# Attention and two MLPs on one core: more working rooms, folded key chunks in turns with the others, and 30 instead of 40 steps of the first MLP beside attention

## The chip, the core and the metric

One core of a Trainium2 chip runs the whole program. The metric is device microseconds of one launch (us). TensorE (PE) multiplies matrices, VectorE (DVE) and ScalarE (ACT) work element by element, GpSimd (POOL) and SyncE (SP) mostly issue DMAs here. Each engine takes its instructions in a fixed order that is set when the program is built.

## What is computed

```python
scores = scale * np.matmul(z, z.transpose(0, 2, 1))     # scale = 1 / S
attn = np.maximum(scores, 0.0) ** 2
x = u * np.matmul(attn, v)                              # (2, 3008, 256) -> (6016, 256)

h = x @ w_in                                            # first MLP, 256 -> 2048 -> 256
P = a[0] + a[1] * h + a[2] * h**2 + a[3] * h**3
Q = 1.0 + np.abs(b[0]) * np.abs(h) + np.abs(b[1]) * h**2
x = (P / (Q + 1e-06)) @ w_out

h = x @ w_in2                                           # second MLP, 256 -> 2048 -> 256
out = (np.maximum(h, 0.0) + alpha * np.minimum(h, 0.0)) @ w_out2
```

The MLPs' weights come in 64-bit type and are converted to 32 bits on the core. Every 32-bit operand is split into a high and a low part, and a product is up to three matmuls (high by high, high by low, low by high).

## The kernel before

**Attention.** There are two batches of 3008 rows. The queries of a batch are taken in six blocks j of 512 (the last has 448), the keys in twelve chunks kp of 256 (the last has 192). One attention step is one chunk of one block: 4 matmuls for the scores (L393, L394), relu and square on ACT into a tile r (L397, L400), a split into high and low part (ACT L118, DVE L121), and 12 matmuls with the values (L437, L446), which follow three steps later. There are 2 x 6 x 12 = 144 steps, counted by st. At a block's end DVE multiplies by u (L482) and the product goes to memory.

**Folding.** The scores are symmetric. In the second batch (`FOLD`) a chunk that lies in an earlier block than its queries is not computed anew: its r was computed when the roles were the other way round. `turn_block` turns such an r with two DMA transposes into a tile xt (L333), `save_turned` writes xt to memory (L341), and `load_turned` fetches it for the later block into a tile xd (L351); ACT and DVE put its two 16-bit halves together (L362, L363). Block j of the second batch has 2j folded chunks, which come first, and turns 10 - 2j others. xt and xd have two buffers each (`XT`, `XD`); tiles r, and the scratch tiles sq, ab and t of the first MLP, share the six buffers of tag "t" (`TT`). A folded chunk has no score matmuls.

**MLPs.** The 6016 rows are taken in 12 groups of 512 (the last has 384), the 2048 hidden columns in 8 parts. One step is one group and one part: 12 matmuls into the hidden tile (L417 to L419) and 12 back (L437, L446), 24 in all, for either MLP. In between, the first MLP has five ACT instructions (L561 to L563, L570, L571) and seven DVE instructions (L565 to L578); the second has two ACT instructions (L621) and two DVE instructions (L622) of half the size, and a split (L118, L121). There are 96 steps of each.

**Weights.** They arrive as 64-bit words, are converted on DVE and ACT (`decode`), and all but 8 tiles of the first MLP's are stored again (wd, L217). Beside attention, a first-MLP step with part 4 to 7 needs two fills of 512 KB from there (L774), which POOL issues. When attention ends, 24 tiles are filled, 16 of them into buffers that the values leave.

**Order.** The main loop takes the attention steps one by one and adds a first-MLP step where `n1_due` says so:

```python
def n1_due(st):
    return max(st + 1 - HEAD, 0) * X1 // (na - HEAD)
```

With HEAD = 36, X1 = 40 and na = 145, 13 steps come in the first batch and 27 in the second. After attention, the other 56 first-MLP steps and 86 second-MLP steps go in turn, spread evenly; 10 second-MLP steps are left for the end. A scheduler then fixes each engine's order, and waits are set where a buffer or a value is needed. All transposes, saves and loads of turned chunks, as well as v, z, u and x, go through the one queue of SP.

Of the kernel before, what the change touches and what calls it, by code (L numbers as in the profile page):

```python
# [11 lines left out]
U16 = mybir.dt.uint16  # L12
# [3 lines left out]
DRAM = bass.MemoryType.DRAM  # L16


BIG, HL, TT, RAW, ZP, XP = 24, 7, 6, 2, 8, 4

XT, XD, AHEAD = 2, 2, 1

FOLD = ((1, 0),)

# [3 lines left out]

LAG_A, LAG_M = 3, 2

HEAD, X1 = 36, 40

RD0, RD = 0.4, 0.55

# [18 lines left out]
def relu2_attention_rational_mlp_prelu_mlp(  # L53
# [15 lines left out]
    nc = tc.nc  # L69
    P = 128  # L70
# [6 lines left out]
    QB = 512  # L77
    NQ = -(-S // QB)
    NK = -(-S // P)
    NKP = NK // 2  # L80
# [15 lines left out]
    zctx = ExitStack()  # L96
    zp = zctx.enter_context(tc.tile_pool(name="zp", bufs=ZP))
    wr = zctx.enter_context(tc.tile_pool(name="wr", bufs=WR))
    xdp = zctx.enter_context(tc.tile_pool(name="xdp", bufs=XD))
    late = {}  # L100

    def raw_tile(nm, early=False):

        if early:
            return big.tile([P, 1024], F32, tag="big", name=nm)
        return tmp.tile([P, 1024], F32, tag="raw", name=nm, bufs=RAW)
# [34 lines left out]
    def load_v(b, kp):  # L141

        if b == 0:
            raw = raw_tile("vraw", True)
        else:
            raw = wr.tile([P, 1024], F32, tag="wr", name="vraw")
        r3 = raw.rearrange("p (c d) -> p c d", c=4)
        r0 = kp * 2 * P
        load_rows(r3, v[b], r0, min(S - r0, 4 * P))
        vraw[b, kp] = r3  # L150
# [97 lines left out]
    def load_z(b, g):  # L248

        raw = raw_tile("zraw", b == 0)  # L250
        n = qn[g]
        nc.sync.dma_start(out=raw[:, 0:n], in_=zt[b, :, g * QB : g * QB + n])
        if n % P:
            nc.sync.dma_start(out=raw[:, n : n + HALF], in_=zt[b, :, S - HALF : S])
            n += HALF
        t = zp.tile([P, QB], F32R, tag="z", name="zA")
        with tc.high_priority(EARLY):
            nc.vector.tensor_copy(t[:, 0:n], raw[:, 0:n])
            nc.vector.tensor_tensor(
                t[HALF:P, 0:n], raw[HALF:P, 0:n], t[HALF:P, 0:n].bitcast(F32), ALU.subtract  # L260
            )
        if (b, g) == (0, 0):
            zB[b, g] = zp.tile([P, QB], F32R, tag="z", name="zB")
            nc.scalar.copy(zB[b, g][HALF:P, 0:n], raw[HALF:P, 0:n])
            nc.vector.tensor_tensor(
                zB[b, g][0:HALF, 0:n], raw[0:HALF, 0:n], t[0:HALF, 0:n].bitcast(F32), ALU.subtract
            )
        zA[b, g] = t


    blocks = [(b, j) for b in range(B) for j in range(NQ)]
# [4 lines left out]
    xd = {}  # L276
# [39 lines left out]
    def folded(b, i, j):  # L316
        return i < j and any(b == fb and i >= f0 for fb, f0 in FOLD)

    turned = {}
    halves = {}  # L320
    unsaved = []

    def turn_block(b, j, kp, r):

        kb, k0 = kp // 2, kp % 2 * 2 * P
        if (b, j, kb) not in turned:
            turned[b, j, kb] = dr.tile([2, QB, QB], U16, name=f"rt{b}_{j}_{kb}")
        x = xdp.tile([P, 8, 2 * P], U16, tag="xt", name="xt", bufs=XT)
        ru = r.bitcast(U16)
        w = 0  # L330
        for i in range(2):
            rows = min(P, S - (2 * kp + i) * P)
            nc.sync.dma_start_transpose(out=x[:, :, w : w + rows], in_=ru[0:rows, i, :])  # L333
            w += rows
        unsaved.append((turned[b, j, kb], k0, w, x))
# [10 lines left out]
    def load_turned(b, j, kp):  # L346
        n = qn[j]
        q0 = kp % 2 * 2 * P
        d = xdp.tile([P, 2, 2, QB], U16, tag="xd", name="xd", bufs=XD)
        for h in range(2):  # L350
            nc.sync.dma_start(  # L351
                out=d[:, h, :, :n],
                in_=turned[b, kp // 2, j][h, q0 : q0 + 2 * P, :n].rearrange("(c p) k -> p c k", p=P),
            )
        halves[b, j, kp] = d
# [13 lines left out]
    def a_scores(b, j, kp):  # L369
# [43 lines left out]
        if folded(b, j, kp // 2):  # L413
            turn_block(b, j, kp, r)
# [16 lines left out]
    def pairs(acc, w, hi, lo, n, first, last, both=2):  # L431

        hi, lo = ([x[i] if type(x) is list else x[:, i, :n] for i in range(2)] for x in (hi, lo))
        for i in range(2):
            for e in range(2):
                for k in range(2):
                    nc.tensor.matmul(  # L437
                        acc[:, e, :n],
                        w[:, k, i, e * P : (e + 1) * P],
                        hi[i],  # L440
                        start=first and i == 0 and k == 0,
                        stop=False,
                    )
        for i in range(both):
            for e in range(2):
                nc.tensor.matmul(  # L446
                    acc[:, e, :n],
                    w[:, 0, i, e * P : (e + 1) * P],
                    lo[i],
                    start=False,  # L450
                    stop=last and i == both - 1,
                )

    def a_values(b, j, kp):
        n = qn[j]
        if kp == 0:

            two = j == 1 and not opened
            acc_a[b, j] = psa.tile([P, ND, QB], F32, tag=f"acc{two:d}", name="acca")
        acc = acc_a[b, j]  # L460
        hi, lo = ahl.pop((b, j, kp))
        vk = vt[b, kp]
        last = kp == NKP - 1
        pairs(acc, vk, hi, lo, n, kp == 0, last, 1 if last else 2)

    def a_u(b, j):
        n = qn[j]
        t = tmp.tile([P, ND, QB], F32, tag="raw", name="ut", bufs=RAW)
        if b == 0 and j < RAW:

            nc.gpsimd.tensor_copy(t[:, 0, 0:1], zA[0, NQ - 1][:, 0:1].bitcast(F32))
        nc.sync.dma_start(
            out=t[:, :, :n],
            in_=ut_in[b, :, j * QB : j * QB + n].rearrange("(e p) s -> p e s", p=P),
        )
        uts[b, j] = t

    def a_end(b, j):
        n = qn[j]
        t = uts.pop((b, j))  # L480
        with tc.high_priority(EARLY):
            nc.vector.tensor_tensor(t[:, :, :n], acc_a[b, j][:, :, :n], t[:, :, :n], ALU.mult)  # L482
        xd[b, j] = dr.tile([P, ND, QB], F32, name=f"xd{b}_{j}")
        nc.sync.dma_start(out=xd[b, j][:, :, :n], in_=t[:, :, :n])
# [185 lines left out]
    def a_stream():  # L670

        pend = []
        coming = [(b, j, kp) for b, j in blocks for kp in range(2 * j) if folded(b, kp // 2, j)]

        def fetch(b, j, kp):
            while coming and len(halves) < AHEAD + folded(b, kp // 2, j) and (
                coming[0][:2] == (b, j) or coming[0][:2] == (b, j + 1) and kp >= NKP - 2
            ):
                load_turned(*coming.pop(0))

        def drain(upto):
            while len(pend) > upto:
                q, kp = pend.pop(0)
                a_values(*q, kp)
                if kp == NKP - 2:
                    a_u(*q)
                if kp == NKP - 1:
                    a_end(*q)

        for q in blocks:  # L690
            b, j = q
            if q == (0, 0):
                load_z(0, 0)
                load_z(0, 1)
                load_v(0, 0)
                split_v(0, 0)
            a_begin(b, j)
            for kp in range(NKP):
                if q == (0, 0) and kp % 2 == 0:
                    for g in {0: (2,), 2: (3, 4), 4: (5,)}.get(kp, ()):  # L700
                        load_z(0, g)
                    if kp + 2 < NKP:
                        load_v(0, kp + 2)
                        split_v(0, kp + 2)
                fetch(b, j, kp)
                a_scores(b, j, kp)
                save_turned(int(folded(b, j, kp // 2)))
                pend.append((q, kp))
                drain(LAG_A)
                if j == NQ - 1 and b + 1 < B:  # L710
                    if kp % 2 == 1:
                        load_z(b + 1, kp // 2)

                k0 = kp - LAG_A - 1 if j == NQ - 1 else kp + NKP - LAG_A - 1
                b1 = b + (j == NQ - 1)
                if (j == NQ - 1 or j == 0) and 0 < b1 < B and k0 % 2 == 0:
                    if 0 <= k0 < NKP:
                        split_v(b1, k0)
                    if 0 <= k0 + 2 < NKP:
                        load_v(b1, k0 + 2)  # L720
                yield
        drain(0)
        yield

# [29 lines left out]
    na = NB * NKP + 1  # L754
# [29 lines left out]
            fill_w(store, jp, big)  # L784

    def n1_due(st):
        return max(st + 1 - HEAD, 0) * X1 // (na - HEAD)

    n1 = nx = 0
    for st in range(na):  # L790
# [79 lines left out]
```

## Time and profile before

| | |
|---|---|
| three runs | 1598.0, 1600.2, 1601.96 us |
| median | 1600.2 us |
| profiled execution | 1600.62 us |
| its span, first to last instruction | 1598.7 us |
| PE busy | 1539.4 us, 96% |
| DVE busy | 1413.9 us, 88% |
| ACT busy | 1172.8 us, 73% |
| DMA: from SP's queue | 93.67 MB, 21.8% of 16 engines |
| DMA: from POOL's queue | 62.94 MB, 13.4% of 16 engines |

The span is the time from the first to the last instruction; the execution has 1.9 us around it. Busy time is a share of the span; matmuls overlap, so a busy PE need not be at its peak. In the windows below, the number in parentheses is that of instructions, and the granted clock is a share of 2.4 GHz.

### The profile page before, as it was taken

What the parts mean: (1) busy time and instruction counts of PE and PEld (TensorE: products, weight loads), DVE (VectorE), ACT (ScalarE), POOL (GpSimd) and SP (SyncE); (2) the same over time, 40 slices, a digit from 0 to 9 for tenths busy, and PEclk for the clock granted to TensorE, in tenths of its full rate; (3) what the DMA queues carried; (4) which work ended last, traced back from release to release, by engine and by line L of the source; (5) the groups of instructions that cost most, each with busy time, mean ns of one, the idle gap of its engine ahead of it and who ended that gap; (6) DMA issues with size and microseconds to landing.
All of it is one profiled execution on the core that took longest, in us unless ns stands there. A gap on an engine that the chain in (4) does not pass through costs nothing.

```text
span 1598.7 us, 18271 instructions
## 1 busy us (share of the span) xinstructions
PE 1539.4 (96%) x6776; PEld 1271.4 (80%) x6776; DVE 1413.9 (88%) x1524; ACT 1172.8 (73%) x1405; POOL 90.5 (6%) x159
## 2 busy tenths in 40 slices
PE   9999999998989889888999999999999999999999
PEld 7887888786768667667788888888888888888888
DVE  8989989896979788999999998999989899998864
ACT  8989988897877878777676676667667676666644
POOL 1021000000001001101200000000000000000000
PEclk9999999998999899999999999999999999999999
DMA  6364132569897878676700010100001000001000
GB/s 203 101 208 148 59 106 73 163 148 228 235 210 209 175 221 157 192 197 214 259 2 27 27 40 1 40 12 28 27 27 40 1 27 28 35 1 40 14 1 23
DMA packets 155784, 157.76 MB, mean 99 GB/s; under 512 B 74016, under 2 KB 124720, under 8 KB 155696
## 3 DMA queue, kind: packets, MB, share of 16 engines
q1 hardware_dynamic: 134928, 93.67, 21.8%
q0 software_dynamic: 20768, 62.94, 13.4%
q8 instruction: 53, 0.87, 0.2%
q14 instruction: 35, 0.29, 0.1%
HBM read 92.94 MB, written 45.74 MB: 87 GB/s over the span
## 4 chain that ended last, share of the span: by engine, by line
PE 67%; DVE 11%; issue 9%; DMA 5%; ACT 5%; POOL 1%; SPq 0%; POOLq 0%; DVEq 0%; ACTq 0%
PE acc L437 18%; PE h L417 9%; PE h L419 9%; PE h L418 9%; PE acc L446 9%; PE acca L437 6%; PE acca L446 3%; DVE alo L121 2%; DMA wd<-dec 1%; PE s L393 1%; PE s L394 1%; DMA xt<-r 1%; PE acce L427 1%; DVE t L577 1%; ACT ahi L118 1%
## 5 line engine op out<-in xcount | busy, mean ns | idle before, releaser
L437 PE MATMUL acc<-ghi,w 128*128 128x512 f32 (+1 forms) x1472 | 365.9, 387 | 1.7 <-DVE ghi L575 1.7
L437 PEld LDWEIGHTS acc<-ghi,w 128*128 128x128 f32 x1472 | 275.3, 188 | 57.3 <-DVE ghi L575 1.6
L437 PE MATMUL acca<-ahi,vt 128*128 128x512 f32 (+1 forms) x1152 | 294.8, 394 | 10.5 <-ACT ahi L118 6.9
L417 PE MATMUL h<-xhi,w 128*128 128x512 f32 (+1 forms) x768 | 295.8, 386 | 4.1 <-DVE t L568 2.1
L418 PE MATMUL h<-xlo,w 128*128 128x512 f32 (+1 forms) x768 | 295.7, 385 | 1.1 <-DVE xlo L121 1.1
L419 PE MATMUL h<-xhi,w 128*128 128x512 f32 (+1 forms) x768 | 295.7, 385 | 0.0
L437 PEld LDWEIGHTS acca<-ahi,vt 128*128 128x128 f32 x1152 | 220.2, 192 | 58.4 <-ACT ahi L118 10.5
L446 PE MATMUL acc<-glo,w 128*128 128x512 f32 (+1 forms) x736 | 199.9, 390 | 10.5 <-DVE glo L578 10.3
L621 ACT ACTIVATE m<-h,sal 128x512 f32<-128x512 f32 (+1 forms) x192 | 127.4, 681 | 111.3 <-PE h L419 109.9
L561 ACT ACTIVATE sq<-h 128x1024 f32<-128x1024 f32 (+1 forms) x96 | 97.1, 1011 | 149.7 <-PE h L419 141.0
L417 PEld LDWEIGHTS h<-xhi,w 128*128 128x128 f32 x768 | 144.1, 188 | 35.4 <-issue 4.1
L446 PEld LDWEIGHTS acc<-glo,w 128*128 128x128 f32 x736 | 137.5, 188 | 41.9 <-DVE glo L578 14.9
L418 PEld LDWEIGHTS h<-xlo,w 128*128 128x128 f32 x768 | 144.1, 188 | 29.4 <-DVE xlo L121 1.9
L419 PEld LDWEIGHTS h<-xhi,w 128*128 128x128 f32 x768 | 144.1, 188 | 27.6
L121 DVE TENSOR_TENSOR glo<-m,ghi 128x1024 fp32r<-128x1024 f32 (+1 forms) x96 | 115.2, 1200 | 55.2 <-PE acc L437 42.0
L622 DVE SCALAR_TENSOR_TENSOR m<-h,sg,m 128x512 f32<-128x512 f32 (+1 forms) x192 | 138.1, 735 | 16.8 <-ACT m L621 15.3
L446 PE MATMUL acca<-alo,vt 128*128 128x512 f32 (+1 forms) x552 | 149.9, 389 | 0.0
L121 DVE TENSOR_TENSOR alo<-r,ahi 128x1024 fp32r<-128x1024 f32 (+2 forms) x103 | 122.9, 1195 | 17.9 <-PE acc L437 8.0
L397 ACT ACTIVATE r<-s 128x512 f32<-128x512 f32 (+1 forms) x184 | 104.2, 595 | 42.5 <-DMA xt<-r 24.3
L575 DVE SCALAR_TENSOR_TENSOR ghi<-t,sc,sq 128x1024 fp32r<-128x1024 f32 (+1 forms) x96 | 120.8, 1258 | 13.1 <-ACT sq L571 7.1
L565 DVE SCALAR_TENSOR_TENSOR ab<-sq,cb,ab 128x1024 f32<-128x1024 f32 (+1 forms) x96 | 120.8, 1258 | 9.9 <-ACT ab L562 9.7
L577 DVE SCALAR_TENSOR_TENSOR t<-t,sc,ab 128x1024 f32<-128x1024 f32 (+1 forms) x96 | 120.9, 1260 | 1.8
(96 smaller groups left out, 2222.8 us busy)
## 6 DMA issues: line engine op xcount, KB each, us to landing
w<-wd POOLq DMA_DIRECT2D x64, 512.0 KB, 4.9
rt<-xt SPq DMA_DIRECT2D x50, 256.0 KB, 3.1
wd<-dec POOLq DMA_DIRECT2D x48, 256.0 KB, 4.2
xd<-rt SPq DMA_DIRECT2D x40, 256.0 KB, 3.6
wraw<-in_moe_w_in_dram POOLq DMA_DIRECT2D x16, 512.0 KB, 4.3
wraw<-in_moe_w_out_dram POOLq DMA_DIRECT2D x16, 512.0 KB, 4.5
x2d<-x SPq DMA_DIRECT2D x11, 512.0 KB, 2.9
xr<-x2d SPq DMA_DIRECT2D x11, 512.0 KB, 3.3
```

What stands on the lines that cost most here:

```text
L121: nc.vector.tensor_tensor(dst_lo, src, dst_hi.bitcast(F32), ALU.subtract)
L397: nc.scalar.activation(r[:, i, :n], s, AF.Relu, scale=1.0 / S)
L417: nc.tensor.matmul(acc, w_hi, hi, start=first, stop=False)
L418: nc.tensor.matmul(acc, w_hi, lo, start=False, stop=False)
L419: nc.tensor.matmul(acc, w_lo, hi, start=False, stop=last)
L437: nc.tensor.matmul(acc[:, e, :n], w[:, k, i, e * P : (e + 1) * P], hi[i], start=first and i == 0 and k == 0, stop=False,)
L446: nc.tensor.matmul(acc[:, e, :n], w[:, 0, i, e * P : (e + 1) * P], lo[i], start=False, stop=last and i == both - 1,)
L565: nc.vector.scalar_tensor_tensor(ab, sq, b1, ab, ALU.mult, ALU.add)
L575: nc.vector.scalar_tensor_tensor(hi, t, a0, sq, ALU.add, ALU.mult)
L577: nc.vector.scalar_tensor_tensor(t, t, a0, ab, ALU.add, ALU.subtract)
L621: nc.scalar.activation(t[:, i], h, AF.Copy, scale=sal[:, f : f + 1])
L622: nc.vector.scalar_tensor_tensor(t[:, i], h, sg[:, f : f + 1], t[:, i], ALU.mult, ALU.max)
```

## The change

The tag "t" gets seven buffers instead of six. Tiles xt and xd share one tag "xx" with six buffers, where each had two. The room for this comes from the memory set apart for POOL's DMA descriptors, which is set to 4096 bytes. In a block of the second batch, folded chunks and others come in turns: block 4, for instance, takes 8, 0, 1, 9, 2, 3, 10, 4, 5, 11, 6, 7 where it took 0 to 11. The first MLP gets 16 steps in the first batch and 14 in the second.

```diff
-BIG, HL, TT, RAW, ZP, XP = 24, 7, 6, 2, 8, 4
-XT, XD, AHEAD = 2, 2, 1
+BIG, HL, TT, RAW, ZP, XP = 24, 7, 7, 2, 8, 4
+XX, AHEAD = 6, 1
+RING = 4096
...
-HEAD, X1 = 36, 40
+HEAD, X0, X1 = 36, 16, 30
...
-    xdp = zctx.enter_context(tc.tile_pool(name="xdp", bufs=XD))
+    xdp = zctx.enter_context(tc.tile_pool(name="xdp", bufs=XX))
...
+    def in_turns(b, j):
+        first = [kp for kp in range(NKP) if folded(b, kp // 2, j)]
+        rest = [kp for kp in range(NKP) if kp not in first]
+        order, nf = [], len(first)
+        while first or rest:
+            ahead = len(first) * (NKP - nf) > len(rest) * nf
+            order.append((first if ahead else rest).pop(0))
+        return order
...
-        x = xdp.tile([P, 8, 2 * P], U16, tag="xt", name="xt", bufs=XT)
+        x = xdp.tile([P, 8, 2 * P], U16, tag="xx", name="xt")
...
-        d = xdp.tile([P, 2, 2, QB], U16, tag="xd", name="xd", bufs=XD)
+        d = xdp.tile([P, 2, 2, QB], U16, tag="xx", name="xd")
...
-            for kp in range(NKP):
+            for pos, kp in enumerate(order[q]):
...
     def n1_due(st):
-        return max(st + 1 - HEAD, 0) * X1 // (na - HEAD)
+        mid = NQ * NKP
+        if st < mid:
+            return max(st + 1 - HEAD, 0) * X0 // (mid - HEAD)
+        return X0 + (st + 1 - mid) * (X1 - X0) // (na - mid)
...
-    nc = _bacc.Bacc("TRN2", target_bir_lowering=False, num_devices=1)
+    nc = _bacc.Bacc("TRN2", target_bir_lowering=False, num_devices=1, dynamic_dma_scratch_size=RING)
```

Where the code asked for the first, last or last but one chunk of a block it now asks for the place in that order, and the fetch of folded chunks follows it too. In the changed kernel the transposes are L346, the saves L354, the loads L364; L565, L567, L568, L575 to L578 are L578, L580, L581, L588 to L591, and L622 is L635.

The SP queue in the second batch's first block, where chunks are only turned, stood so before (xt is the turned chunk, r the scores, rt the memory it is saved to, xd a loaded chunk):

```order
L333 DMA_TRANSPOSE xt_3259<-r_3245 128x8x128 x2
L333 DMA_TRANSPOSE xt_3291<-r_3276 128x8x128 x2
L341 DMA rt1_0_2_3185<-xt_3259 64x8x256 x2
L341 DMA rt1_0_3_3290<-xt_3291 64x8x256 x2
L333 DMA_TRANSPOSE xt_3322<-r_3308 128x8x128 x2
L351 DMA xd_3583<-rt1_0_1_3069 128x2x512
L341 DMA rt1_0_3_3290<-xt_3322 64x8x256
L333 DMA_TRANSPOSE xt_3396<-r_3381 128x8x128 x2
L341 DMA rt1_0_3_3290<-xt_3322 64x8x256
L341 DMA rt1_0_4_3395<-xt_3396 64x8x256 x2
```

and stands so now:

```order
L346 DMA_TRANSPOSE xt_3385<-r_3370 128x8x128 x2
L346 DMA_TRANSPOSE xt_3416<-r_3402 128x8x128 x2
L354 DMA rt1_0_3_3384<-xt_3385 64x8x256 x2
L346 DMA_TRANSPOSE xt_3448<-r_3433 128x8x128 x2
L354 DMA rt1_0_3_3384<-xt_3416 64x8x256 x2
L346 DMA_TRANSPOSE xt_3496<-r_3482 128x8x128 x2
L354 DMA rt1_0_4_3447<-xt_3448 64x8x256 x2
L364 DMA xd_3513<-rt1_0_1_3199 128x2x512 x2
L346 DMA_TRANSPOSE xt_3531<-r_3516 128x8x128 x2
L354 DMA rt1_0_4_3447<-xt_3496 64x8x256 x2
```

Before, two chunks are transposed, then both are saved, or a transpose stands behind the save of the chunk before it. Now the transposes of a further chunk stand between a chunk's transposes and its saves.

DVE in the middle of the MLPs, a piece of some twelve instructions before (L567 to L578 are of one first-MLP step; each pair of L622, with a glo<-m, is a second-MLP step):

```order
L567 TENSOR_TENSOR t<-t,h_8251 128x1024
L622 SCALAR_TENSOR_TENSOR m<-h_8295,sg,m 128x512
L622 SCALAR_TENSOR_TENSOR m<-h_8304,sg,m 128x512
L568 SCALAR_TENSOR_TENSOR t<-t,sc,h_8251 128x1024
L575 SCALAR_TENSOR_TENSOR ghi<-t,sc,sq 128x1024
L576 SCALAR_TENSOR_TENSOR ab<-ab,ghi 128x1024
L622 SCALAR_TENSOR_TENSOR m<-h_8330,sg,m 128x512
L622 SCALAR_TENSOR_TENSOR m<-h_8339,sg,m 128x512
L577 SCALAR_TENSOR_TENSOR t<-t,sc,ab 128x1024
L578 TENSOR_TENSOR glo<-t,sq 128x1024
L121 TENSOR_TENSOR glo<-m,ghi 128x1024 x2
```

and a like piece now:

```order
L578 SCALAR_TENSOR_TENSOR ab<-sq,cb,ab 128x1024
L580 TENSOR_TENSOR t<-t,h_8475 128x1024
L635 SCALAR_TENSOR_TENSOR m<-h_8522,sg,m 128x512
L635 SCALAR_TENSOR_TENSOR m<-h_8531,sg,m 128x512
L581 SCALAR_TENSOR_TENSOR t<-t,sc,h_8475 128x1024
L588 SCALAR_TENSOR_TENSOR ghi<-t,sc,sq 128x1024
L589 SCALAR_TENSOR_TENSOR ab<-ab,ghi 128x1024
L590 SCALAR_TENSOR_TENSOR t<-t,sc,ab 128x1024
L591 TENSOR_TENSOR glo<-t,sq 128x1024
L123 TENSOR_TENSOR glo<-m,ghi 128x1024
L578 SCALAR_TENSOR_TENSOR ab<-sq,cb,ab 128x1024
L580 TENSOR_TENSOR t<-t,h_8556 128x1024
```

In the piece before, two second-MLP steps stand within a first-MLP step; in the piece now one stands there and the next first-MLP step follows. There were 56 to 86 of them in this stretch, now there are 66 to 86. On POOL, 52 fills are issued instead of 64.

## Rows read from the trace of the kernel before

**Rows 1.** The page: busy time of each engine; the DMA engines' share in 40 slices.

```profile
PE 1539.4 (96%) x6776; PEld 1271.4 (80%) x6776; DVE 1413.9 (88%) x1524; ACT 1172.8 (73%) x1405; POOL 90.5 (6%) x159
...
DMA  6364132569897878676700010100001000001000
```

**Rows 2.** Windows: us, busy us (instructions) per engine, granted clock, DMA share, GB/s.

```profile
141.80:340.10 198.30, 192.48 (x850) 159.34 (x849) 181.51 (x193) 175.16 (x228) 12.93 (x23) 0.99 0.31 97
340.10:421.20 81.10, 73.46 (x311) 59.62 (x311) 64.24 (x65) 64.39 (x79) 6.51 (x11) 0.94 1.00 223
421.20:490.90 69.70, 63.42 (x269) 50.96 (x269) 58.61 (x62) 56.32 (x69) 4.71 (x8) 0.95 0.90 209
490.90:575.10 84.20, 74.60 (x309) 59.17 (x307) 70.26 (x78) 61.78 (x72) 9.46 (x15) 0.94 0.83 205
575.10:641.00 65.90, 61.33 (x262) 48.48 (x262) 60.57 (x65) 53.77 (x62) 5.92 (x11) 1.00 0.75 175
641.00:710.00 69.00, 60.39 (x248) 46.68 (x248) 64.07 (x76) 52.42 (x61) 6.59 (x11) 0.98 0.64 183
710.00:781.00 71.00, 63.91 (x282) 54.38 (x281) 63.46 (x64) 52.82 (x58) 10.48 (x19) 0.95 0.68 215
...
800.00:850.00 50.00, 49.88 (x219) 40.70 (x219) 48.47 (x47) 33.54 (x38) 0.00 (x0) 1.00 0.00 1
850.00:1400.00 550.00, 550.00 (x2426) 454.63 (x2425) 506.77 (x492) 368.50 (x425) 0.00 (x0) 1.00 0.08 26
```

**Rows 3.** Windows of the stall in the second batch's first block.

```profile
371.00:381.00 10.00, 10.00 (x45) 8.26 (x44) 4.62 (x5) 9.11 (x11) 1.06 (x2) 1.00 1.28 202
381.00:391.00 10.00, 2.62 (x9) 1.84 (x8) 5.83 (x7) 2.20 (x4) 0.00 (x0) 0.66 0.95 236
391.00:401.00 10.00, 10.00 (x39) 8.07 (x37) 6.90 (x9) 6.73 (x11) 0.72 (x1) 0.83 0.90 203
```

**Rows 4.** Chain of waits, 371 to 401 us: start us, us, what.

```profile
370.20 5.43 DMA xt<-r
...
376.34 7.40 DMA rt<-xt
...
385.16 3.53 DMA xt<-r
...
388.80 0.61 ACT r L397
```

**Rows 5.** Waits, second batch: who for whom, us in total, times, longest.

```profile
ACT r L397 <- DMA xt<-r: 24.3, 5, 8.7
PE s L393 <- ACT r L397: 23.7, 7, 7.4
```

**Rows 6.** Waits of the SP queue, second batch.

```profile
SPq L351 <- DVE rr L363: 75.2, 22, 7.7
...
SPq L341 <- DMA xt<-r: 44.8, 23, 7.5
```

**Rows 7.** DMA: 440.2 to 444.6, 446.0 to 449.0, and 782.8 to 799 us.

```profile
DMA packets 3380, 0.86 MB, mean 195 GB/s; under 512 B 3379, under 2 KB 3379, under 8 KB 3379
...
DMA packets 1917, 0.82 MB, mean 273 GB/s; under 512 B 571, under 2 KB 1917, under 8 KB 1917
...
DMA packets 1804, 6.10 MB, mean 377 GB/s; under 512 B 174, under 2 KB 430, under 8 KB 1803
```

**Rows 8.** DVE by line, 850 to 1400 us: count, busy us, mean ns, idle before.

```profile
L622 DVE SCALAR_TENSOR_TENSOR m<-h,sg,m 128x512 f32<-128x512 f32 x124 | 90.1, 746 | 1.3 <-ACT m L621 0.3
L121 DVE TENSOR_TENSOR glo<-m,ghi 128x1024 fp32r<-128x1024 f32 x62 | 75.7, 1222 | 31.8 <-PE acc L437 29.0 <-ACT ghi L118 2.7
L577 DVE SCALAR_TENSOR_TENSOR t<-t,sc,ab 128x1024 f32<-128x1024 f32 x40 | 51.2, 1280 | 0.7
...
L567 DVE TENSOR_TENSOR t<-t,h 128x1024 f32<-128x1024 f32 x40 | 48.6, 1215 | 0.9 <-ACT t L563 0.9
```

**Rows 9.** The page's DMA issues: count, KB each, median us to landing.

```profile
w<-wd POOLq DMA_DIRECT2D x64, 512.0 KB, 4.9
```

More of the change, by code (lines that the diff above doesn't have):

```diff
@@ L317, in folded @@
         return i < j and any(b == fb and i >= f0 for fb, f0 in FOLD)
+    def in_turns(b, j):
[6 more added lines that the diff above has]
+        return order
+    order = {q: in_turns(*q) for q in blocks}
     turned = {}
@@ L455, in a_values @@
         n = qn[j]
-        if kp == 0:
+        if kp == order[b, j][0]:
             two = j == 1 and not opened
@@ L462, in a_values @@
         vk = vt[b, kp]
-        last = kp == NKP - 1
-        pairs(acc, vk, hi, lo, n, kp == 0, last, 1 if last else 2)
+        first, last = kp == order[b, j][0], kp == order[b, j][-1]
+        pairs(acc, vk, hi, lo, n, first, last, 1 if kp == NKP - 1 else 2)
     def a_u(b, j):
@@ L672, in a_stream, with fetch @@
         pend = []
-        coming = [(b, j, kp) for b, j in blocks for kp in range(2 * j) if folded(b, kp // 2, j)]
-        def fetch(b, j, kp):
+        coming = [(*q, kp) for q in blocks for kp in order[q] if folded(q[0], kp // 2, q[1])]
+        def fetch(b, j, kp, pos):
             while coming and len(halves) < AHEAD + folded(b, kp // 2, j) and (
-                coming[0][:2] == (b, j) or coming[0][:2] == (b, j + 1) and kp >= NKP - 2
+                coming[0][:2] == (b, j) or coming[0][:2] == (b, j + 1) and pos >= NKP - 2
             ):
@@ L684, in drain @@
                 a_values(*q, kp)
-                if kp == NKP - 2:
+                if kp == order[q][-2]:
                     a_u(*q)
-                if kp == NKP - 1:
+                if kp == order[q][-1]:
                     a_end(*q)
@@ L704, in a_stream @@
                         split_v(0, kp + 2)
-                fetch(b, j, kp)
+                fetch(b, j, kp, pos)
                 a_scores(b, j, kp)
@@ L710, in a_stream @@
                 if j == NQ - 1 and b + 1 < B:
-                    if kp % 2 == 1:
-                        load_z(b + 1, kp // 2)
-                k0 = kp - LAG_A - 1 if j == NQ - 1 else kp + NKP - LAG_A - 1
+                    if pos % 2 == 1:
+                        load_z(b + 1, pos // 2)
+                k0 = pos - LAG_A - 1 if j == NQ - 1 else pos + NKP - LAG_A - 1
                 b1 = b + (j == NQ - 1)
```

## The prediction

> **What bounds the kernel now.** I read the page's engine shares first [rows 1]: TensorE (PE) is busy 96% of the span, so the question is where its missing microseconds lie. The windows [rows 2] cut the span at the program's own borders: the attention blocks end at 141.8 (third), 340.1 (sixth, end of the first batch), 421.2, 490.9, 575.1, 641, 710 and 781 us (the six blocks of the second batch); the rest is MLPs alone. Between 850 and 1400 us PE is busy all the time and does 2426 matmuls in 550 us, so one of 512 columns costs 550/2426 = 0.2267 us. That is my unit; a 448-column one is taken as 448/512 of it, 0.198 us. A first-MLP step has 24 matmuls: 5.44 us.
>
> From the code, the second batch's attention has 190, 182, 174, 166 and 158 matmuls of 512 columns and 150 of 448 in its six blocks: 870 x 0.2267 + 150 x 0.198 = 227 us. Beside it run 27 first-MLP steps (40 less the 13 due before), 146.9 us. That is 374 us of PE work in a stretch of 781.0 - 340.1 = 440.9 us: 67 us are lost. The blocks from 141.8 to 340.1 lose little: 380 x 0.2267 + 190 x 0.198 + 13 x 5.44 = 194.5 of 198.3 us.
>
> Where the 67 us go: between 381 and 391 us PE is busy 2.62 us, and the granted clock, after PE stood still, is 0.66, then 0.83 on average, a mix of its levels 1.2 and 2.4 GHz [rows 3]; the two windows hold 48 matmuls where 88 would fit, so one stall costs some 9 us with its slow restart. The chain of waits through it [rows 4] is a transpose, a save, a further transpose that needed the saved room, and then ScalarE (ACT), which may write its tile r only when that transpose has read the old one. PE waits 23.7 us for such scores, ACT 24.3 us for transposes [rows 5]; the SP queue stands 44.8 us before saves of transposes not landed, and 75.2 us before loads whose buffer DVE still reads [rows 6]. So it is rooms (two for transposes, two for loads, six t tiles), not an engine's rate.
>
> **Rooms.** The six t tiles become seven, and the 2 + 2 rooms become six in common. The printed SP order shows the result in block (1,0): a transpose of the next chunk stands between a transpose and its save. What remains is the DMA engines' own work. While mostly transposes ran they moved 195 GB/s, while mostly saves ran 273 [rows 7]; a half chunk is 0.262 MB, so a turned chunk costs 2 x 1.34 + 2 x 0.96 = 4.6 us. Thirty of them are 138 us; 60 loads at the rate of the saves 58; 30 weight fills, 11 weight conversions with their stores (twice the bytes) and some 18 tiles of u and x are 70 times 0.524 MB, 97 us at the 377 GB/s of the fills after attention [rows 7] (1.39 us each). Sum 293 us, an estimate from these rates. The DMA shares of the blocks [rows 2] times their lengths give 356 us before, less 12 fills 340: the upper bound, if a share of 1.00 means full. I lean to the rates: a share of 1.28 stands in the window before the stall [rows 3], so 1.00 is no ceiling.
>
> The Trainium skill (DMA: Bandwidth & Descriptors, Latency and other measured facts) states an effective 261 GB/s for DMA transposes. The rows here, 195 GB/s, do not reach it. By the Trainium skill's figure the turned chunks would cost 30 x 2 x 0.34 = 20 us less than in the sum of 293, and rival 1 below would end 16 us earlier.
>
> **Key chunks in turns.** Loads (folded chunks) and transposes (the others) are spread over a block instead of loads first. No work is added. It is worth what it takes off the two queues above, in one sum with the rooms.
>
> **30 steps, not 40.** The first batch gets 16 instead of 13: PE +16.3 us. Its windows from 141.8 have DVE 181.5 of 198.3 us busy [rows 2]. In 850 to 1400 us the ten groups of DVE rows, four of them shown [rows 8], add up to 534.5 us and its busy time is 506.8 [rows 2], since instructions overlap: factor 0.948. A first-MLP step has four DVE instructions like L577 and three like L567, 4 x 1.28 + 3 x 1.22 = 8.8, times 0.948 8.3 us. Three more make 206 of 214.6 us, 96%; I add 3 us of loss. Sum +19.5 us.
>
> The second batch gets 14 instead of 27. PE needs 374 - 70.7 = 303 us; DVE had 381 us [rows 2], less 13 x 8.3 leaves 273; ACT has 341 before and falls too; DMA 293 to 340. From below: with the 2% loss of the first batch's stretch it would take 309 us. From above: the four blocks without the great stalls (421.2 to 490.9 and 575.1 to 781) took 275.6 us for 506 x 0.2267 + 150 x 0.198 + 18 x 5.44 = 242.4 us of PE work, 1.137 times it, which gives 345 us. I take 335, 1.105 times, nearer to the upper row, because DMA, DVE and PE now lie within a tenth of each other. 335 - 441 = -106 us.
>
> MLPs alone: 66 instead of 56 first-MLP steps, so PE +54.4 us. Is DVE the limit? In 850 to 1400 us there are 40 first-MLP and 62 second-MLP steps [rows 8]; DVE takes 506.8/40 = 12.67 us for 1 and 1.55 of them, PE 13.75. After the change it is 1 to 86/66 = 1.30; a second-MLP step costs DVE (2 x 0.746 + 1.222) x 0.948 = 2.57 us, so DVE takes 12.03 us and PE 2.303 x 5.44 = 12.53: 96%. From 800 to 850 us DVE was busy 48.47 of 50 us, 97%, with PE at 49.88 [rows 2]. So I add 3 us, +57.4 in all.
>
> **Small ring for POOL's DMAs.** Nothing shows its use. Below: a gain has no source, so 0. Above: the last eight fills come in one go when attention's pools close; at 377 GB/s they take 11 us, and one at a time eight times the 4.9 us median of such a fill [rows 9], 39: +28 us. I take 0, the end to which the rows with many fills at once [rows 7] are nearest, since the fills before the change already follow one another slowly, behind PE's releases. Twelve fills fewer (52 for 64) lie beside other work.
>
> **Sum** against the profiled execution, 1600.6 us (span 1598.7 and 1.9 around it; the median of the runs is 1600.2): +19.5 - 106 + 57.4 = -29, **1571.5 us**.
>
> **Rivals.**
> 1. *The DMA engines are full.* Blocks one to three of the second batch had shares 1.00, 0.90 and 0.83: 81.1 + 62.7 + 69.9 = 213.7 us, less 8 fills 203. The other three take 146.7 us of PE work times 1.10, 161. Together 364 us, -77, and the sum is 0: 1600.6. For it: share 1.00 in block one. Against: the profile's DMA slices of this batch mostly stand at 6 to 8 tenths [rows 1], and fills alone moved 377 GB/s.
> 2. *The chain of transposes still sets the pace* (the slow one): a save still stands before a later transpose in one queue. Then the first three blocks keep their 235 us, and the batch takes 396: -45 + 77 = +32, 1632. It decides from 203 us for these blocks, 8.5 us for each of their 24 turned chunks; now it is 9.8, and the transfers are 4.6. Against: the new rooms are just what the chain waited for.
> 3. *DVE bounds the MLPs.* If in its fixed order it cannot pass the 92.1% of 850 to 1400 us, a group takes 12.03/0.921 = 13.06 us, 0.53 more than PE; 66 times is 35, and the time 1603.5. Against it stands the window 800 to 850 [rows 2].
>
> That the change does not do what it says is excluded for order and counts by the printed rows; that the rooms do nothing is rival 2.
>
> **Numbers.** Forecast 0.70, rivals 0.12, 0.10 and 0.08. A difference under 0.3% (4.8 us) cannot be told from none. The forecast's own bounds are 1545 (batch at 309) and 1582 (345). The range 1550 to 1604 takes in rivals 1 and 3 and leaves out rival 2 and the tails. Faster: nearly all of 0.70 and some of rivals 1 and 3, 0.75; same 0.09; slower 0.16.
>
> **What would show it.** The second batch's attention should take 320 to 350 us, with no stall of PE behind a transpose over 4 us and the wait of ACT for transposes under 10 us; the six blocks each under 65 us. The stretch after attention should take 870 to 885 us with DVE at 95% and PE at 99% or more. Wrong would be: first three blocks over 200 us in all (rivals 1 and 2, told apart by idle DMA), or PE waits for glo and for t in the MLPs (rival 3).

## The result and the profile after

The changed kernel takes 1560.26 us in the median of three runs (1556.2 to 1561.91), before 1600.2: a ratio of 0.9746 with a 95% interval of 0.9711 to 0.9782. Its profiled execution is the fastest of the three, 1556.2 us with a span of 1554.4, so the two traces differ by 44.3 us where the medians differ by 39.9. Forecast were 1571.5 us, in a range of 1550 to 1604.

Windows of the changed kernel, cut at the ends of its attention blocks as [rows 2] are: the last three blocks of the first batch together, the six blocks of the second, these six as a whole, all MLPs after attention, and a middle piece of those. Columns as in [rows 2].

```profile
141.50:356.70 215.20, 209.88 (x930) 172.25 (x930) 205.33 (x215) 191.34 (x244) 14.68 (x26) 1.00 0.30 94
356.70:433.20 76.50, 66.80 (x273) 52.08 (x271) 53.48 (x60) 62.19 (x79) 6.70 (x12) 0.96 1.09 235
433.20:478.10 44.90, 44.23 (x193) 35.96 (x194) 36.89 (x44) 37.58 (x49) 3.61 (x6) 1.00 1.07 255
478.10:533.90 55.80, 54.94 (x242) 44.79 (x241) 47.07 (x53) 48.72 (x59) 5.77 (x10) 1.00 1.13 278
533.90:590.10 56.20, 54.44 (x234) 43.19 (x233) 50.71 (x62) 46.83 (x57) 7.00 (x12) 1.00 1.03 258
590.10:638.30 48.20, 46.81 (x207) 38.49 (x206) 45.81 (x57) 42.68 (x49) 3.76 (x7) 1.00 0.87 257
638.30:680.70 42.40, 41.95 (x197) 36.48 (x196) 40.84 (x44) 32.97 (x37) 7.08 (x13) 1.00 0.71 210
...
356.70:680.70 324.00, 309.18 (x1339) 250.99 (x1338) 274.80 (x312) 270.97 (x324) 33.91 (x60) 0.99 1.00 249
680.70:1554.40 873.70, 870.15 (x3911) 726.41 (x3909) 809.38 (x792) 579.07 (x677) 4.76 (x9) 1.00 0.09 29
...
750.00:1355.00 605.00, 605.00 (x2659) 497.08 (x2658) 584.07 (x555) 413.08 (x472) 0.00 (x0) 1.00 0.08 25
```

| stretch | before | forecast | after |
|---|---|---|---|
| up to the end of the first batch | 340.1 us | +19.5 | 356.7 us, +16.6 |
| second batch's attention | 441 us | -106 | 324.0 us, -117 |
| MLPs after attention | 817.6 us | +57.4 | 873.7 us, +56.1 |
| span | 1598.7 us | -29 | 1554.4 us, -44.3 |

The second batch holds 303 us of PE work, by the count of the prediction, so 21 us are lost there where 67 were. Most of that is lost in the first block: its 273 matmuls are 61.9 us of PE work and it took 76.5 us, 14.6 more. Only the first block still has a granted clock below 1.00. Its waits are of the old kind, and shorter. The first fence is from who waited for whom in the second batch (total us, times, longest), and answers to [rows 5]; the second is from SP's own waits, and answers to [rows 6].

```profile
PE s L406 <- ACT r L410: 10.8, 5, 4.3
...
ACT rr L375 <- DMA xd<-rt: 6.1, 3, 2.7
...
ACT r L410 <- DMA xt<-r: 4.3, 1, 4.3
```

```profile
SPq L354 <- DMA xt<-r: 19.3, 12, 5.9
...
SPq L364 <- DVE rr L376: 7.1, 4, 4.6
```

PE's wait for scores fell from 23.7 to 10.8 us, ACT's for transposes from 24.3 to 4.3, SP's before loads whose buffer is still read from 75.2 to 7.1. The longest wait of PE behind such a transpose was 7.4 us and is 4.3.

### The profile page after: what moved, and what is told of

Read it like the earlier page. It is cut to its first block, busy times and chain, and to the rows that moved or that the text cites. A ratio compares the mean times of both kernels' runs of the same rounds, so it can differ in the third digit from the quotient of the medians.

```text
span 1554.4 us, 18172 instructions
## 1 busy us (share of the span) xinstructions
PE 1528.6 (98%) x6776; PEld 1263.3 (81%) x6776; DVE 1418.1 (91%) x1524; ACT 1169.1 (75%) x1405; POOL 82.7 (5%) x147
## 3 DMA queue, kind: packets, MB, share of 16 engines
q0 software_dynamic: 19040, 56.64, 12.2%
## 4 chain that ended last, share of the span: by engine, by line
PE 73%; DVE 9%; ACT 6%; issue 5%; DMA 4%; SPq 2%; POOL 1%; DVEq 0%; ACTq 0%; POOLq 0%
PE acc L450 20%; PE h L430 10%; PE h L432 10%; PE h L431 10%; PE acc L459 10%; PE acca L450 6%; PE acca L459 3%; DVE alo L123 2%; ACT ahi L120 1%; DMA xd<-rt 1%; PE s L406 1%; PE acce L440 1%; SPq L346 1%; ACT r L410 1%; PE s L407 1%
## 5 line engine op out<-in xcount | busy, mean ns | idle before, releaser
L450 PE MATMUL acca<-ahi,vt 128*128 128x512 f32 (+1 forms) x1152 | 288.0, 388 | 6.0 <-ACT ahi L120 4.5
L450 PEld LDWEIGHTS acca<-ahi,vt 128*128 128x128 f32 x1152 | 215.6, 189 | 53.6 <-ACT ahi L120 9.8
L634 ACT ACTIVATE m<-h,sal 128x512 f32<-128x512 f32 (+1 forms) x192 | 124.6, 687 | 51.3 <-PE h L432 51.0
L635 DVE SCALAR_TENSOR_TENSOR m<-h,sg,m 128x512 f32<-128x512 f32 (+1 forms) x192 | 135.3, 734 | 16.7 <-ACT m L634 16.0
L578 DVE SCALAR_TENSOR_TENSOR ab<-sq,cb,ab 128x1024 f32<-128x1024 f32 (+1 forms) x96 | 120.8, 1258 | 14.3 <-ACT ab L575 14.1
L588 DVE SCALAR_TENSOR_TENSOR ghi<-t,sc,sq 128x1024 fp32r<-128x1024 f32 (+1 forms) x96 | 120.9, 1259 | 9.5 <-ACT sq L584 3.1
L590 DVE SCALAR_TENSOR_TENSOR t<-t,sc,ab 128x1024 f32<-128x1024 f32 (+1 forms) x96 | 121.0, 1261 | 2.5
L459 PEld LDWEIGHTS acca<-alo,vt 128*128 128x128 f32 x552 | 103.5, 188 | 21.3 <-DVE alo L123 1.6
```

Of the source, the lines that this page charges most:

```text
L450: nc.tensor.matmul(acc[:, e, :n], w[:, k, i, e * P : (e + 1) * P], hi[i], start=first and i == 0 and k == 0, stop=False,)
L459: nc.tensor.matmul(acc[:, e, :n], w[:, 0, i, e * P : (e + 1) * P], lo[i], start=False, stop=last and i == both - 1,)
L578: nc.vector.scalar_tensor_tensor(ab, sq, b1, ab, ALU.mult, ALU.add)
L588: nc.vector.scalar_tensor_tensor(hi, t, a0, sq, ALU.add, ALU.mult)
L590: nc.vector.scalar_tensor_tensor(t, t, a0, ab, ALU.add, ALU.subtract)
L634: nc.scalar.activation(t[:, i], h, AF.Copy, scale=sal[:, f : f + 1])
```

## The experiments

A room is one buffer of a tag, as in the prediction. Three theories were set against each other: R, the rooms end the stalls, and moving steps is neutral; S, the steps taken from the second batch free tiles and engines, and that ends them; T, the turns do it, by spreading loads and transposes. For each run the table gives the median, the ratio to the kernel before with its 95% interval, the second batch's length in the profile, and that length less its PE work (374 us with 40 steps, 303 with 30, 249 with 20), called the loss. Steps that lag over a border make a loss uncertain by some 5 us. The row of the changed kernel has its own three runs.

| kernel | median, us | ratio | second batch | loss |
|---|---|---|---|---|
| before | 1599 to 1602 | 1 | 441 us | 67 |
| changed | 1560.3 | 0.9746 (0.9711 to 0.9782) | 324 us | 21 |
| e1: rooms and turns, 40 steps | 1560.3 | 0.9734 (0.9691 to 0.9777) | 402 us | 28 |
| e2: 30 steps only | 1599.1 | 0.9990 (0.9968 to 1.0013) | 365 us | 62 |
| e3: changed, no turns | 1586.9 | 0.9898 (0.9862 to 0.9933) | 356 us | 53 |
| e4: changed, old rooms | 1580.4 | 0.9860 (0.9826 to 0.9895) | 350 us | 47 |
| e5: changed, six t tiles | 1570.7 | 0.9823 (0.9789 to 0.9857) | 340 us | 37 |
| e6: changed, 2 + 2 rooms | 1568.2 | 0.9806 (0.9767 to 0.9846) | 333 us | 30 |
| e7: changed, 20 steps | 1621.1 | 1.0129 (1.0094 to 1.0164) | 301 us | 52 |
| e8: changed, five steps in block one | 1573.6 | 0.9837 (0.9804 to 0.9871) | 343 us | 40 |
| f1: changed, earlier fetch | 1568.8 | 0.9785 (0.9739 to 0.9830) | 340 us | 37 |
| f2: e8 with earlier fetch | 1570.9 | 0.9812 (0.9777 to 0.9847) | 334 us | 31 |
| f3: before, small ring | 1600.7 | 0.9997 (0.9980 to 1.0014) | 441 us | 67 |
| f5: e1 with earlier fetch | 1559.9 | 0.9750 (0.9714 to 0.9786) | 399 us | 25 |

### e1: rooms and turns without moving steps

```diff
-        mid = NQ * NKP
-        if st < mid:
-            return max(st + 1 - HEAD, 0) * X0 // (mid - HEAD)
-        return X0 + (st + 1 - mid) * (X1 - X0) // (na - mid)
+        return max(st + 1 - HEAD, 0) * X1 // (na - HEAD)
```

(with X1 = 40.)

> The changed kernel with the 40 evenly spread first-MLP steps of before: rooms and turns alone. Theory R (rooms end the stalls, moving steps is neutral): the second batch's attention needs 374 us of PE work and takes 395 to 410, the MLPs alone go back to 818 us, the time is 1560 to 1575 us, and no PE stall behind transposes is over 4 us. Theory S (the thirteen steps less leave tiles, DVE and ACT free, and that ends the stalls): 1590 us or more, with stalls of 5 us and more as before. DVE speaks for a value in between: it needs some 381 us of such a batch.

1560.25 us: the whole gain is there without a step moved. Windows of e1, the first block of the second batch and the whole of it:

```profile
337.10:407.90 70.80, 70.80 (x310) 57.61 (x310) 64.62 (x65) 66.45 (x82) 6.50 (x11) 1.00 1.00 235
337.10:739.40 402.30, 385.54 (x1671) 311.41 (x1671) 379.05 (x403) 338.03 (x394) 43.53 (x77) 1.00 0.87 224
```

The first block, with 310 matmuls, is shorter than the changed kernel's with 273, and PE never stands still in it. PE's longest wait in the whole batch is 3.1 us. DVE is busy 94% of the batch. Theory S falls. No run has only the rooms or only the turns with 40 steps, so their shares are known for 30 steps alone (e3 and e4).

### e2: the steps alone

In the kernel before, `n1_due` as in the change, with 16 and 30:

```diff
-        return max(st + 1 - HEAD, 0) * X1 // (na - HEAD)
+        mid = NQ * NKP
+        if st < mid:
+            return max(st + 1 - HEAD, 0) * X0 // (mid - HEAD)
+        return X0 + (st + 1 - mid) * (X1 - X0) // (na - mid)
```

> The kernel before with 16 and 14 steps instead of 40 evenly, rooms and chunk order as before: the steps alone. Theory R: the first three blocks of the second batch are still paced by the two rooms of transposes and keep 215 to 235 us, the time is 1595 to 1630 us. Theory S: 1560 to 1575 us, second batch at 335 us or less.

No difference that can be measured: the batch loses 62 us, about as much as before, in part in other places. The first three blocks took 194 us, less than I gave them, and the fourth 72.7 (65.9 before). Waits of e2's second batch:

```profile
PE h L417 <- DVE t L568: 17.7, 5, 9.4
ACT rr L362 <- DMA xd<-rt: 15.7, 9, 3.4
ACT rr L362 <- DVE t L577: 15.5, 6, 3.8
...
ACT t L563 <- DMA xt<-r: 13.6, 2, 10.1
...
DVE t L567 <- ACT t L563: 12.2, 3, 9.7
...
PE s L393 <- ACT r L397: 10.3, 10, 3.3
```

PE's longest stall, 9.4 us, is still of the kind of [rows 4]. ACT's L563, which writes a t tile for the first MLP, waited 10.1 us for a transpose, DVE waited 9.7 us for it, and PE for DVE; here the tile is a scratch tile of the MLP, where it was r before. Besides, ACT's instruction rr L362, which opens a folded chunk, now waits for its load and for a t tile, and behind it in ACT's and DVE's fixed orders stands what PE needs.

### e3: no turns

```diff
-            ahead = len(first) * (NKP - nf) > len(rest) * nf
+            ahead = len(first) > 0
```

> The changed kernel with folded chunks first in each block again. Theory R: turns are worth little once there are rooms: 1556 to 1568 us. Theory T (the even load on SP and the DMA engines is what counts): 1580 us or more, with PE stalls in blocks two to four, where the transposes stand together at a block's end.

1586.9 us, 27 above the changed kernel: Theory T, not R, for this part. Waits in e3's second batch, and below them SP's own:

```profile
ACT rr L375 <- DMA xd<-rt: 40.1, 9, 10.5
...
PE h L430 <- DVE t L581: 14.8, 4, 7.3
...
PE acca L450 <- ACT ahi L420: 7.8, 1, 7.8
```

```profile
SPq L346 <- ACT ahi L120: 51.4, 7, 25.3
```

With rooms, but folded chunks first, ACT waits 40.1 us for loads (6.1 in the changed kernel): a block begins with chunks that all need one, while SP is held up to 25.3 us in front of a transpose. Blocks two to four took 50.0, 68.0 and 62.4 us where the changed kernel has 44.9, 55.8 and 56.2.

### e4, e5, e6: the rooms

e4 has both edits, e5 the first only, e6 the other two only:

```diff
-BIG, HL, TT, RAW, ZP, XP = 24, 7, 7, 2, 8, 4
+BIG, HL, TT, RAW, ZP, XP = 24, 7, 6, 2, 8, 4
...
-        x = xdp.tile([P, 8, 2 * P], U16, tag="xx", name="xt")
+        x = xdp.tile([P, 8, 2 * P], U16, tag="xt", name="xt", bufs=2)
...
-        d = xdp.tile([P, 2, 2, QB], U16, tag="xx", name="xd")
+        d = xdp.tile([P, 2, 2, QB], U16, tag="xd", name="xd", bufs=2)
```

> The changed kernel with the rooms of before (six t tiles, two tiles each for transposes and loads); steps, turns and the small descriptor ring stay. Theory R: 1590 us or more, SP waits for its rooms, and PE has stalls over 5 us again. Theories S or T: 1560 to 1572 us.

> The changed kernel with six t tiles instead of seven; the six shared rooms stay. If the shared rooms of transposes and loads hold the gain of the rooms (20 us between the changed kernel and the one with all rooms of before), this stays at 1558 to 1566 us; if the seventh t tile holds it, it goes to 1574 us or more.

> The changed kernel with two rooms for transposes and two for loads again; the seven t tiles stay. The other half of the same question: 1574 to 1582 us if the shared rooms hold the gain, 1558 to 1566 us if the t tile does, something between if each holds a part.

e4 lost 20 us of the 40, less than R wanted and more than S or T; PE's longest stall in its batch was 5.2 us again. e5 and e6 lost 10 and 8 (e6's interval just touches the changed kernel's), so by the medians the two kinds of room hold about half of it each, and each shows in its own wait. But the order of the instructions changed with the rooms too: e5's second block, for one, has 197 matmuls and its third 238, where the changed kernel has 193 and 242. As e8 below shows that a changed order can cost as much, how much of the 10 and 8 us is the rooms' own is not shown. SP's waits in e4:

```profile
SPq L364 <- DVE rr L376: 44.2, 17, 7.2
SPq L354 <- DMA xt<-r: 38.2, 23, 7.7
```

SP's waits in e6 (two rooms for loads, two for transposes):

```profile
SPq L364 <- DVE rr L376: 43.9, 15, 12.2
...
SPq L346 <- DMA rt<-xt: 13.7, 10, 3.5
```

Waits of ACT and PE in e5 (six t tiles):

```profile
PE s L406 <- ACT r L410: 14.5, 9, 6.1
ACT r L410 <- DVE t L590: 12.7, 5, 3.8
...
ACT rr L375 <- DVE t L590: 11.4, 5, 4.3
ACT r L410 <- DMA xt<-r: 8.8, 4, 4.9
```

The 44 us of SP before loads come back with the 2 + 2 rooms and not with the t tile (7.9 us in e5). In e6, ACT's wait for loads rose to 17.7 us from 6.1, and the last block, which has most folded chunks, took 51.3 us where the changed kernel has 42.4. In e5, ACT waits for a t tile that a first-MLP step (DVE L590) or a transpose still reads.

### e7: 20 steps

```diff
-HEAD, X0, X1 = 36, 16, 30
+HEAD, X0, X1 = 36, 16, 20
```

> The changed kernel with 20 first-MLP steps beside attention, 16 and 4. The second batch then needs some 249 us of PE work. If the DMA engines set a floor near the estimate of 293 us, less 10 fills 280 (transposes and saves at the rates of the rows), the batch takes 280 to 300 us and the time is 1590 to 1610 us; if there is no such floor, 265 us and 1560 us. In the MLPs alone there are 76 first-MLP to 86 second-MLP steps: DVE would need as long as PE (11.6 us a group by both), and PE should wait for DVE for the first time, in all for 5 to 20 us there.

1621.1 us, above both ranges. The second batch came to 301.3 us, just above the 280 to 300 that a DMA floor would give; its PE work is 249. Windows of e7: the second batch, and 600 us of the MLPs:

```profile
358.00:659.30 301.30, 261.32 (x1094) 207.84 (x1093) 193.93 (x239) 220.55 (x271) 28.10 (x48) 0.94 1.01 243
700.00:1300.00 600.00, 588.92 (x2538) 472.04 (x2537) 579.58 (x543) 402.58 (x456) 4.25 (x8) 1.00 0.09 31
```

DVE and ACT are busy under three quarters of that batch, and the DMA share and rate (1.01 at 243 GB/s) are those of the changed kernel's whole batch (1.00 at 249). That speaks for the DMA engines, but one wait of PE of 12.8 us for a copy on SP's queue (zB<-zA) is in it too, so a floor of the DMA engines alone is not shown. In the MLPs the miss was in size. They took 960.3 us, 32 more than 873.7 + 54.4, where 5 to 20 were expected: 2538 matmuls in 600 us are 575 us of PE work, and DVE was busy 96.6%. PE's own waits there are nearly all for DVE (first three lines), and its weight loads (PEld) waited for the same DVE instructions:

```profile
PE acc L459 <- DVE glo L591: 6.2, 11, 2.0
PE h L430 <- DVE m L635: 4.7, 14, 1.5
PE h L430 <- DVE t L581: 3.3, 2, 2.3
```

```profile
PEld h L430 <- DVE m L635: 14.2, 30, 2.0
...
PEld acc L459 <- DVE glo L591: 12.6, 15, 2.5
```

That is 14.2 us of PE and 26.8 us of the weight loads, which overlap; no wait accounts for the whole of the 32. In the changed kernel DVE is busy 96.5% (584.07 of 605 us) and PE does 2659 matmuls, one every 0.2275 us, close to its pace of 0.2267. No wait of PE is listed in its MLPs, and its weight loads wait 1.5 us for DVE. So the change stands just short of the point where DVE takes over.

### e8, f1, f2, f5: can the rest be had?

e8 puts five of the 14 steps into the first block:

```diff
-HEAD, X0, X1 = 36, 16, 30
+HEAD, X0, X1, FRONT = 36, 16, 30, 5
...
-        return X0 + (st + 1 - mid) * (X1 - X0) // (na - mid)
+        if st < mid + NKP:
+            return X0 + (st + 1 - mid) * FRONT // NKP
+        return X0 + FRONT + (st + 1 - mid - NKP) * (X1 - X0 - FRONT) // (na - mid - NKP)
```

f1, f2 and f5 fetch folded chunks one earlier, in the changed kernel, e8 and e1:

```diff
-XX, AHEAD = 6, 1
+XX, AHEAD = 6, 2
```

> The changed kernel with five of the second batch's 14 first-MLP steps in its first block and nine in the other five. If that block is bound by its ten turned chunks on SP's queue and the DMA engines (76.5 us in the changed kernel, 70.8 us and PE busy throughout with 40 steps), the added steps cost nothing there and the time falls to 1545 to 1553 us; if PE or the tiles bound the block, it stays at 1556 to 1564 us.

> The changed kernel with folded chunks fetched one chunk earlier (AHEAD = 2), three of the six rooms at most. If what is left of the losses in blocks two to six are loads that come late on SP's queue behind transposes (ACT waits 6.1 us for them there), 1550 to 1556 us; if rooms are short again, since loads now hold three of the six, 1565 us or more.

> The kernel with five steps in the second batch's first block, and the same earlier fetch. If that kernel lost in block two (67.7 us where the changed kernel has 44.9) only because the load of its second folded chunk stood behind four pairs of transposes and saves, block two falls to 55 us or less and the time to 1545 to 1558 us; if it is bound there by DMA or PE, it stays at 1570 to 1577 us.

> The kernel with rooms, turns and 40 even steps, and the earlier fetch. There ACT waits 10.4 us for loads in the second batch. If they are late for SP's queue, 1550 to 1557 us; otherwise 1558 us or more.

e8 missed. Its first two blocks:

```profile
356.10:428.90 72.80, 71.01 (x306) 56.25 (x305) 65.01 (x65) 63.74 (x79) 5.46 (x10) 1.00 1.00 234
428.90:496.60 67.70, 55.40 (x231) 44.06 (x230) 45.87 (x55) 50.01 (x64) 7.03 (x12) 0.92 1.09 239
```

The first did as expected: 33 matmuls more than the changed kernel's in 3.7 us less. The second lost far more, 67.7 us for 44.9. Pieces of its chain of waits from 462 to 490 us (start us, us, what):

```profile
467.09 3.20 SPq L346
471.03 3.26 SPq L354
474.34 7.95 DMA xd<-rt
...
485.58 3.78 PE acca L450 x8
```

SP's order put the load of the block's second folded chunk behind the transposes and saves, and PE stood 10.7 us for it. With the earlier fetch (f2) that wait is 4.9 us and the block 60.7: better, not the 55 that was expected, and the whole is as slow, 1570.9. In the changed kernel the earlier fetch gained nothing that can be seen. f1's median lies in the range expected if rooms are short again, and SP waited 12.2 us before loads whose buffer DVE still reads (7.1 in the changed kernel), while ACT's wait for loads fell from 6.1 to 1.4 us; but its four runs go from 1557.4 to 1571.1 us and its interval overlaps the changed kernel's, so a loss is not shown. With 40 steps (f5) the time is that of e1, though ACT's wait for loads fell from 10.4 to 1.5 us. What sets the second block's length in f2 stays open. No run beat the changed kernel; e1 and f5 are level with it.

### f3: the small ring alone

```diff
-    nc = _bacc.Bacc("TRN2", target_bir_lowering=False, num_devices=1)
+    nc = _bacc.Bacc("TRN2", target_bir_lowering=False, num_devices=1, dynamic_dma_scratch_size=4096)
```

> The kernel before with the descriptor memory of POOL's DMAs at 4096 bytes and nothing else. If the ring never fills, the time is that of before within 0.3%; if POOL waits for room, the eight fills at the end of attention land up to 28 us later and PE waits there for weights.

A ratio of 0.9997: the small ring costs nothing here, and the memory it leaves pays for the rooms.

## Why the prediction was right, and where not

**What bounds.** "So it is rooms ..., not an engine's rate" was half of it. With 30 steps, the rooms are worth 20 us once the turns are in (e4 against the changed kernel), the turns 27 us once the rooms are in (e3); over e2 the turns alone gain 19 us (e4) and the rooms alone 12 (e3). The prediction put the turns into one sum with the rooms, so its total held, but it named only the rooms as the cause. What the turns remove, once the rooms are in, is another wait than the one that [rows 4] and [rows 5] led me to: ACT and DVE, in fixed order, before a folded chunk whose load is not there (40.1 us of ACT in e3, 6.1 in the changed kernel). With the old rooms the same wait fell from 15.7 us (e2) to 6.2 (e4).

**Rooms.** The waits of [rows 6] went as said. The estimate of 293 us of DMA work was not contradicted: the batch took 324 us with 303 us of PE work, and 301 us in e7, where ten fills fewer make the estimate 280. Whether it is a floor is not shown. The bound of 340 from the shares is refuted by these two. Rival 1, with 364 us for the batch, fell with it.

**Steps.** Moving ten of them is neutral by e1 and e2, and the sum said nearly that: its +19.5 and +57.4 were +16.6 and +56.1. The second batch took 324 us instead of 335: the factor 1.105 on PE work was 1.07. This is the term that was too careful, and it makes most of the 15 us between the forecast and the profiled execution.

**Wrong details.** "The six blocks each under 65 us" failed for the first: 76.5. I counted its steps' PE work and left out how long its turned chunks take. SP's queue filled 88.5% of the DMA engines' time between 360 and 434 us (first fence below). In that first block the changed kernel issued 22 transposes. e1 issued 20 in 70.8 us, with five MLP steps and PE busy throughout, and e7 18 in 59.1 us, with 203 matmuls (second fence: its first block). That is 3.3 to 3.5 us for each transpose in all three, which a pace of the transposes would explain; but in e1 PE work alone explains the length too, and whether the DMA engines or the order on SP set such a pace, no run separates.

```profile
q1 hardware_dynamic: 34109, 13.07, 88.5%
q0 software_dynamic: 1416, 4.27, 22.8%
```

```profile
358.00:417.10 59.10, 49.34 (x203) 38.88 (x201) 28.41 (x34) 40.40 (x54) 4.91 (x9) 0.91 1.10 236
```

Two more signs just missed. One stall of PE behind a transpose was 4.3 us, over the 4 that were allowed. DVE was busy 92.6% of the stretch after attention, where 95% was said; only its middle has 96.5%.

**Rival 2** (the chain keeps its pace) failed: the first three blocks took 177 us, under its point of 203; even with the old rooms and order, fewer steps brought them to 194 (e2), so its price was too high as well. **Rival 3** (DVE bounds the MLPs) did not come true here, but begins not far beyond: PE is not held with DVE at 96.5% in the changed kernel, above the 92.1% that the rival took as DVE's limit, and the MLPs lose 32 us in e7, where DVE would need as long as PE.

**The transposes' rate.** The Trainium skill (DMA: Bandwidth & Descriptors, Latency and other measured facts) gives 261 GB/s for transposes with a non-contiguous middle dimension, measured on one kernel. The trace does not agree: the one row that holds mostly transposes has 195 GB/s [rows 7].

## What to carry to other kernels

When one queue carries both what frees a tile and what fills one, look at how producers and consumers lie in the order before buying rooms: here spreading them over the block was worth at least as much as the extra buffers, and needed no memory. Moving work from a stretch that stalls to one that is full gained nothing here, neither in the kernel before (e2) nor in the changed one (against e1). The stretch that receives it has a limit that could be read off beforehand from the second engine's time per group: with 20 steps DVE was forecast to need as long as PE, and there the MLPs began to lose, though more than was forecast.

## What was not expected

DVE can run at 96.5% of the time for 605 us without holding PE back, whose pace there is 0.2275 us a matmul against 0.2267 with DVE at 92.1%. At 96.6% it did hold PE back by 25 of 600 us in e7: the busy share hardly tells the two apart, the work asked of DVE does.

A small move of MLP steps (e8) changes the static order of all engines, and it cost 13 us, more than either kind of room by itself. In f1, which moves the fetches, the median is 8 us higher, but that is not clear of the noise. So a difference of 10 us between two such kernels need not come from the part that was meant to change.
